# A fused linear attention and gated feed-forward kernel: the written-out order of all engines' operations replaced by another one

## The chip, the cores and the metric

The kernel runs on one core of one Trainium2 chip. The metric is the device time of one execution in microseconds. The core has five engines with a queue of instructions each: PE (TensorE, matrix products from SBUF into PSUM), DVE (VectorE) and ACT (ScalarE), which do elementwise work and empty PSUM, POOL (GpSimd), which here issues the loads, and SP (SyncE), which issues the stores. An engine works through its own queue in order and waits where an operand isn't ready or a buffer isn't free. PSUM has eight banks of 128 x 512 fp32 values.

## The reference

Eight batches with eight heads, 576 positions, head size 64; model width 512, hidden width 1024.

```python
kv = np.einsum('bhsd,bhse->bhde', k, v)
out = np.einsum('bhsd,bhde->bhse', q, kv)
rms = np.sqrt(np.mean(out * out, axis=-1, keepdims=True) + 1e-06)
x = (out / rms * g_norm)            # then heads side by side: (8, 576, 512)
h = np.maximum(x @ w_in, 0.0)       # (8, 576, 1024)
conv_out = cw[0] * h[s-1] + cw[1] * h[s] + cw[2] * h[s+1]   # along the positions
gate = 1.0 / (1.0 + np.exp(-conv_out))
y = (h * gate) @ w_out              # (8, 576, 512)
```

## The kernel before

The program is a list of small operations. `ORDER` (L59) is a string of some 850 tokens; the loop at L779 issues them one after the other, and the last loop (L786) ties every instruction to the one before it on its engine. So the string is the order of each engine's queue. A token is a name, its numbers after dots, and after `@` the buffer or PSUM bank that it takes. Numbers are mostly batch `b`, pair of heads' tiles `u` and half of the positions `s`; for the feed-forward part batch `b` and hidden block `f` (0 to 7); for the output a pair of batches `p` and a block `m` of 128 rows (0 to 8).

PE's operations:
- `fi.n.512` (L283): n fillers, products of zeros with 512 columns that nobody reads. `ct` transposes the constants.
- `qt` (L425) transposes q in 64x64 blocks; `kv` and `kz` (L395, L473) form k-by-v for all heads; `ot` and `ox` (L454, L492) form q-by-kv. All these use PE's array as 64x64 tiles.
- `on` (L524) and `oq` (L531) sum the squares over a head, `on` with the full 128x128 array, `oq` with 64x64 tiles. For batches 4 to 7 this is done by `ss` (L560, 128x32 tiles) for two batches at once, and `sp` (L587, 32x128 tiles) spreads the factors back.
- `hk` (half of the contraction), `hs` and `hm` (L652, L624, L608) form the hidden layer; `cv` (L701) does batch 0's convolution of four hidden blocks as products.
- `om.p.m.f0.4` (L727) adds four hidden blocks to an output block: `om.p.m.0.4` is the first half, `om.p.m.4.4` the second. `oh.3.8.c` (L753) does the last block in two halves of the columns.

What empties PSUM or prepares operands, on ACT or DVE:
- `caa`/`cad` (L392, L389): batch 0's inputs from fp32 to bf16, on ACT or DVE. `qa`/`qd` (L448, L451) copy the transposed q, `kva`/`kvd` (L419, L422) copy kv, `ea`/`ed` (L736, L741) copy an output block, `eh`/`dh` (L765, L770) copy a half of the last one; the first name of each is ACT's, the second DVE's.
- ACT: `sq` squares, `oc` copies o, `nl` and `ln` take the reciprocal root, `rp`, `rh`, `re` are the relu, `sg` and `sc` the sigmoid. Going from a root to a sigmoid or back loads a table (L227).
- DVE: `mo` and `mu` scale by root and g, `sl` splits the factors in bf16 parts, `ta` (two multiplications), `aa`, `ab` form the convolution, `mg` gates. `pl`, `ps`, `pn`, `pc`, `pg`, `dg` prepare constants.

Transfers: `Lq`, `Lk`, `Lv`, `Li`, `Lo` load q, k, v, w_in and w_out through POOL, with a cast; a load into a buffer waits until its last reader is done. k and v have two buffers each, q three. `st` and `sh` store a row block or a half of one through SP; `tq` transposes q by a transfer, and `kx` swaps the halves of kv, both through SP as well. `pre` starts the loads of batch 0 on SP and ACT.

Dependencies between engines come from the data and the buffers alone; each PSUM bank is named in the token, so a product that takes a bank waits for the operation that empties it.

Of the kernel before, what the change touches and what calls it, by code (L numbers as in the profile page):

```python
# [89 lines left out]
nl.3.0.0@4 hs.3.4.1@7 rh.3.4.1 hs.3.1.1@6 rh.3.1.1 on.3.1.0@4 nl.3.1.0@5 mo.3.0.0 hs.3.6.1@7 rh.3.6.1 hs.2.6.0@6  # L90
# [40 lines left out]
mg.7.1.3 om.3.3.0.4@2 om.3.3.4.4 ed.3.3@5 st.3.3 mg.7.1.2 om.3.1.0.4@1 om.3.2.0.4@7 om.3.0.4.4 om.3.2.4.4 ed.3.2@0  # L131
st.3.2 ed.3.0@2 st.3.0 om.3.1.4.4 ea.3.1@1 st.3.1 om.3.4.0.4@0 om.3.5.0.4@4 om.3.6.0.4@3 om.3.7.0.4@6 om.3.7.4.4
ed.3.7@4 om.3.5.4.4 ea.3.5@3 st.3.5 om.3.4.4.4 ed.3.4@5 st.3.4 st.3.7 om.3.6.4.4 ea.3.6@0 st.3.6 oh.3.8.1@1 eh.3.8.1@2
sh.3.8.1 oh.3.8.0@0 eh.3.8.0@1 sh.3.8.0
"""


@with_exitstack
def kernel(
# [46 lines left out]
    T = {}  # L186
# [260 lines left out]
    @op  # L447
    def qa(b, u, s): qc(0, b, u, s)  # L448
# [376 lines left out]
```

## Time and profile before

| | us |
|---|---|
| median of three runs | 177.79 (177.78 to 178.52) |
| span of the profiled execution, first to last instruction | 175.6 |
| PE busy | 167.9 |
| DVE busy | 149.5 |
| ACT busy | 148.9 |

In the lines of the profile a group is: source line, engine, operation, result and operands, count. Times are in microseconds from the start of the span. In a timeline a line has the start, the length and in brackets the idle time of the engine before it, with what ended it; the length includes the emptying of the engine's pipeline, so that two neighbours can overlap, and the distance between starts is the price of one in a row of many. The chain of waits follows the execution back from its last instruction; its pieces don't overlap. PEld is the load of a product's stationary operand.

### The profile page before, as it was taken

Reading aid. Unit: us, or ns where it says so; the run is one execution under the profiler, and the core shown is the slowest. Engines: PE = TensorE matmul, PEld = TensorE weight load, DVE = VectorE, ACT = ScalarE, POOL = GpSimd, SP = SyncE. Lnnn points to the kernel's source line nnn. Section 1 sums busy time; section 2 is a strip of 40 time slices with the busy share of each in tenths; the row PEclk is TensorE's granted clock in tenths of the full one; section 3 lists DMA queues with packets and bytes.
Section 4 is the critical chain, followed back from the end, with each engine's and each line's share of the span. In section 5 each row is a group of like instructions: output and inputs, shape, how many; then the busy total and the mean of one; then the engine's idle time right before and its main releaser. Section 6 shows DMA issues by size and latency. Waiting matters only on the chain.

```text
span 175.6 us, 5070 instructions
## 1 busy us (share of the span) xinstructions
PE 167.9 (96%) x2097; PEld 100.0 (57%) x2114; DVE 149.5 (85%) x290; ACT 148.9 (85%) x268; POOL 22.2 (13%) x35
## 2 busy tenths in 40 slices
PE   7979999999999999999999999999999999999992
PEld 2334766676447677644467764444877744444451
DVE  2796638899688899999999998989999999999950
ACT  2368899999978999999999998999999967676721
POOL 3094512200603013030000000000000000000000
PEclk9999999999999999999999999999999999999999
DMA  5999999999999999999999050330310003064486
GB/s 159 392 323 207 207 207 207 208 208 209 207 241 230 227 207 207 170 182 197 258 181 161 14 134 0 119 123 0 119 63 0 0 0 116 13 239 175 179 304 237
DMA packets 25911, 29.11 MB, mean 166 GB/s; under 512 B 6036, under 2 KB 20384, under 8 KB 25888
## 3 DMA queue, kind: packets, MB, share of 16 engines
q0 software_dynamic: 13296, 14.50, 49.2%
q1 hardware_dynamic: 12048, 13.11, 26.2%
q10 hardware_dynamic: 544, 1.18, 1.7%
q8 instruction: 16, 0.26, 0.6%
q14 instruction: 7, 0.06, 0.1%
HBM read 32.52 MB, written 9.44 MB: 239 GB/s over the span
## 4 chain that ended last, share of the span: by engine, by line
PE 76%; DVE 12%; ACT 5%; DMA 3%; issue 3%; ACTq 0%; DVEq 0%
PE banks L732 32%; PE banks L628 14%; PE banks L613 9%; PE banks L658 4%; DMA stg<-in_v_dram 3%; PE banks L460 3%; DVE h L722 2%; PE banks L708 2%; ACT taps L698 2%; PE banks L402 2%; PE banks L593 2%; PE banks L433 1%; PE banks L528 1%; DVE taps L681 1%; PE banks L286 1%
## 5 line engine op out<-in xcount | busy, mean ns | idle before, releaser
L732 PE MATMUL banks<-w_out_sb,h 128*128 128x512 bf16 x267 | 62.8, 379 | 1.2 <-issue 0.6
L698 ACT ACTIVATE taps<-taps,cw 128x576 bf16<-128x576 bf16 (+1 forms) x44 | 40.6, 958 | 5.7 <-DVE taps L692 5.5
L732 PEld LDWEIGHTS <-h 128*128 128x128 bf16 x280 | 26.2, 98 | 30.0 <-issue 1.1
L628 PE MATMUL banks<-x,w_in_sb 128*128 128x288 bf16 (+2 forms) x256 | 34.2, 286 | 0.0
L640 ACT ACTIVATE h<-banks 128x288 bf16<-128x288 f32 (+2 forms) x80 | 29.5, 460 | 0.3 <-PE banks L658 0.2
L628 PEld LDWEIGHTS <-w_in_sb 128*128 128x128 bf16 x256 | 24.4, 98 | 7.8 <-issue 0.8
L722 DVE TENSOR_TENSOR h<-h,taps 128x1152 bf16<-128x1152 bf16 (+1 forms) x24 | 22.8, 952 | 1.2 <-ACT taps L698 1.2
L687 DVE TENSOR_TENSOR taps<-taps 128x1152 bf16<-128x1152 bf16 (+1 forms) x22 | 21.5, 978 | 0.5
L509 ACT ACTIVATE sq<-banks 128x576 bf16<-128x576 f32 (+2 forms) x32 | 20.8, 691 | 1.1 <-PE banks L460 1.1
L692 DVE TENSOR_TENSOR taps<-taps,h 128x1152 bf16<-128x1152 bf16 (+1 forms) x22 | 21.4, 972 | 0.3
L681 DVE TENSOR_SCALAR taps<-h,cw 128x576 bf16<-128x576 bf16 (+1 forms) x44 | 18.7, 424 | 0.6 <-ACT h L665 0.5
L682 DVE TENSOR_SCALAR taps<-h,cw 128x576 bf16<-128x576 bf16 (+1 forms) x44 | 18.4, 418 | 0.0
L738 ACT ACTIVATE row<-banks 128x512 f32<-128x512 f32 x23 | 13.5, 597 | 5.7 <-PE banks L732 4.2
L658 PE MATMUL banks<-x,w_in_sb 128*128 128x288 bf16 (+2 forms) x128 | 17.7, 286 | 0.1
L613 PE MATMUL banks<-x,w_in_sb 128*128 128x288 bf16 x128 | 16.9, 286 | 0.0
L556 DVE SCALAR_TENSOR_TENSOR x<-banks,cw,rs 128x576 bf16<-128x576 f32 (+2 forms) x16 | 13.0, 816 | 3.9 <-ACT rs L545 3.6
L658 PEld LDWEIGHTS <-w_in_sb 128*128 128x128 bf16 x128 | 12.0, 98 | 4.4 <-issue 0.5
L227 ACT ACT_TABLE_LOAD x10 | 12.8, 1283 | 2.0 <-issue 1.8
L613 PEld LDWEIGHTS <-w_in_sb 128*128 128x128 bf16 x128 | 12.3, 98 | 3.7 <-issue 0.2
L443 DVE COPY qT<-banks 128x1152 bf16<-128x1152 bf16 (+2 forms) x13 | 8.8, 681 | 5.7 <-PE banks L433 5.7
L545 ACT ACTIVATE rs<-banks,eps_sb 128x576 f32<-128x576 f32 (+2 forms) x16 | 11.8, 740 | 1.1 <-PE banks L528 1.1
L599 DVE SCALAR_TENSOR_TENSOR x<-o,cw,banks 128x576 bf16<-128x576 f32 (+2 forms) x16 | 12.1, 810 | 0.7 <-PE banks L593 0.5
(89 smaller groups left out, 162.9 us busy)
## 6 DMA issues: line engine op xcount, KB each, us to landing
out_dram<-row SPq DMA_DIRECT2D x35, 256.0 KB, 2.3
q_sb<-in_q_dram POOLq DMA_DIRECT2D x6, 576.0 KB, 17.9
k_sb<-in_k_dram POOLq DMA_DIRECT2D x6, 576.0 KB, 14.5
v_sb<-in_v_dram POOLq DMA_DIRECT2D x6, 576.0 KB, 17.9
stg<-in_v_dram ACTq DMA_DIRECT2D x2, 576.0 KB, 6.2
stg<-in_k_dram SPq DMA_DIRECT2D x4, 288.0 KB, 6.9
w_in_sb<-in_moe_w_in_dram POOLq DMA_DIRECT2D x2, 512.0 KB, 9.9
w_out_sb<-in_moe_w_out_dram POOLq DMA_DIRECT2D x1, 1024.0 KB, 15.5
```

The costliest lines, as they stand in the source:

```text
L509: nc.scalar.activation(T["sq", b, u, s], T["o", b, u, s], AX.Square)
L613: nc.tensor.matmul(ps[:, s, :HS], w_in_sb[:, t, f * P:(f + 1) * P], T["x", b][:, t, c0:c1], start=(t == 0), stop=(t == NT - 1))
L628: nc.tensor.matmul(ps, w_in_sb[:, t, f * P:(f + 1) * P], T["x", b][:, t, c0:c1], start=(t == 0), stop=(t == NT - 1))
L640: nc.scalar.activation(h, fr, AX.Relu)
L658: nc.tensor.matmul(T[at], w_in_sb[:, t, f * P:(f + 1) * P], T["x", b][:, t, c0:c1], start=(t == 0), stop=(t == NT - 1))
L681: nc.vector.tensor_scalar_mul(tap[:, 0, f % 2, :n, 8:8 + S], h[:, f], cw[:, f:f + 1])
L682: nc.vector.tensor_scalar_mul(tap[:, 1, f % 2, :n, :S], h[:, f], cw[:, 2 * NF + f:2 * NF + f + 1])
L687: nc.vector.tensor_add(tap[:, 1, :, :n, :S], tap[:, 0, :, :n, 7:7 + S], tap[:, 1, :, :n, 1:1 + S])
L692: nc.vector.tensor_add(y, y, span(b, n)[:, 2 * j:2 * j + 2])
L698: nc.scalar.activation(y, y, AX.Sigmoid, scale=cw[:, NF + f:NF + f + 1])
L722: nc.vector.tensor_mul(h, h, tap_of(b, j)[:, 1, :, :n, :S])
L732: nc.tensor.matmul(T["om", p, m], h[:, f, m * P:(m + 1) * P], w_out_sb[:, f, :], start=(f == 0), stop=(f == NF - 1))
```

## The change

`ORDER` is replaced as a whole, and two buffers are made by whichever token comes first instead of by the one with number 0. The set of operations is the same but for these:

- 22 copies and casts change engine. To ACT: `caa.q.0.0`, `caa.v.0.0`, `caa.k.1.0`, `caa.v.3.0`, `caa.q.0.1`, `qa.0.0.0`, `qa.0.1.0`, `kva.3.0.2`, `ea.0.1`, `ea.2.8`, `ea.3.0`, `ea.3.2`, `ea.3.3`, `ea.3.7`. To DVE: `cad.v.1.0`, `cad.q.1.0`, `qd.0.0.1`, `ed.1.0`, `ed.1.1`, `ed.1.4`, `ed.3.5`, `dh.3.8.0`.
- `oq` becomes `on` for 1.0.0 and 1.0.1, and `on` becomes `oq` for 1.1.0 and 3.0.0.
- The fillers go from 37 to 42.

The order of the loads, of the stores and of the transposing transfers is new too, and so are the banks and buffers. The diff, cut to the front, the loads of k for batches 5 and 6, and the end:

```diff
-pre@0,1 af cad.q.0.0@0 cad.v.0.0@0 fi.10.512@0 qt.0.0.0@2 qd.0.0.0@0 gt.k.1.0 Li.0.4 fi.9.512@0 ct@0 Lq.1.0.2@1
-Lk.1.0.2@0 Lv.1.0.2@1 Li.4.4 ps pg fi.4.512@1 cad.k.1.0@1 caa.v.1.0 caa.k.0.0 kv.0.0.1@4 kva.0.0.1@0 ot.0.0.0@6 pc
-cad.v.3.0 cad.k.2.0 fi.2.512@0 cad.k.3.0 caa.q.1.0 qt.0.1.0@2 qd.0.1.0@1 sq.0.0.0@0 oq.0.0.0@4 fi.2.512@0 dg.1
-caa.v.2.0 kv.0.1.1@0 fi.2.512@2 nl.0.0.0@0 kva.0.1.1 ot.0.1.0@4 sq.0.1.0@1 cad.q.0.1 qt.0.0.1@2 qa.0.0.1 fi.2.512@0
-oq.0.1.0@0 nl.0.1.0@1 mo.0.0.0@0 cad.q.1.1 qt.0.1.1@6 qd.0.1.1 mo.0.1.0 ot.0.0.1@2 sq.0.0.1@2 ot.0.1.1@6 fi.1.512@0
-sq.0.1.1@3 oq.0.0.1@0 nl.0.0.1@2 fi.1.512@4 fi.1.512@4 hk.0.1.0.0@4 hk.0.1.0.1 rp.1.0@0 on.0.1.1@0 nl.0.1.1@3
+pre@0,1 af pl ps caa.q.0.0@0 caa.v.0.0@0 fi.20.512@0 qt.0.0.0@0 qa.0.0.0@0 pn caa.k.0.0@0 cad.v.1.0 fi.8.512@2 ct@0 pg
+caa.k.1.0 pc gt.k.1.0 Li.0.4 caa.v.2.0 fi.4.512@1 kv.0.0.1@0 Lq.1.0.2@1 kva.0.0.1@0 cad.q.1.0 caa.v.3.0 fi.2.512@2
+ot.0.0.0@0 dg.0 qt.0.1.0@2 Lk.1.0.2@1 dg.2 sq.0.0.0@0 cad.k.2.0 qa.0.1.0@1 Lv.1.0.2@1 cad.k.3.0 fi.3.512@4 oq.0.0.0@4
+nl.0.0.0@0 dg.3 fi.1.512@6 kv.0.1.1@2 Lq.1.2.2 dg.1 kva.0.1.1 mo.0.0.0@0 caa.q.0.1 Li.4.4 fi.2.512@6 ot.0.1.0@2
+cad.q.1.1 sq.0.1.0@0 fi.1.512@4 qt.0.0.1@4 Lv.1.2.2 qd.0.0.1 oq.0.1.0@6 qt.0.1.1@0 nl.0.1.0@1 Lk.1.2.2 ot.0.0.1@4
+qd.0.1.1 sq.0.0.1@0 ot.0.1.1@0 mo.0.1.0 sq.0.1.1@1 fi.1.512@6 oq.0.0.1@6 nl.0.0.1@0 on.0.1.1@2 nl.0.1.1@1 mo.0.0.1
+hk.0.1.0.0@6 Lq.2.0.4@0 hk.0.2.0.0@7 hk.0.2.0.1 hk.0.1.0.1 mo.0.1.1 rp.2.0@0 hk.0.3.0.0@2 hk.0.3.0.1 rp.1.0
+hk.0.1.1.0@3 Lo.0.8 rp.3.0 hk.0.0.0.0@4 hk.0.2.1.0@5 hk.0.2.1.1 hk.0.1.1.1 rp.2.1 hk.0.0.1.0@7 Lk.2.0.4@0 hk.0.0.1.1
...
-hs.3.3.0@5 rh.3.3.0 rh.3.7.0 kv.4.0.2@0 kvd.4.0.2@1 hs.3.0.0@2 hs.3.3.1@6 mg.1.1.1 Lk.5.0.4@0 rh.3.3.1 hs.3.2.1@7
...
-Lv.5.0.4@1 Lq.7.0.4@1 Lk.6.0.4@1 oc.4.0.0@6 hs.2.7.1@3 rh.2.7.1 ot.4.0.1@0 sq.4.0.1@1 oc.4.0.1@7 kv.5.0.2@4 ta.2.2.0@1
...
+kv.3.0.2@2 sq.2.0.0@0 ed.0.0@3 hk.1.3.0.1 kva.3.0.2@0 Lk.6.0.4@1 on.2.0.0@4 rh.1.3.0 hs.2.5.1@2 nl.2.0.0@0 Lv.5.0.4@1
...
+mo.3.0.0 on.3.1.0@2 rh.3.1.1 hs.3.6.1@5 nl.3.1.0@1 hs.2.3.0@4 mo.3.1.0 kv.4.0.2@2 qt.4.1.0@0 kvd.4.0.2@0 Lk.5.0.4@0
...
+oc.4.0.1@0 aa.2.2.1 om.0.7.4.4 sq.4.0.0@1 hs.3.7.1@2 oc.4.0.0@1 ed.0.7@4 ot.4.1.1@0 rh.2.6.0 kv.5.0.2@6 ta.2.2.0@1
...
+ss.6.6.2@0 ab.4.2.3 ss.7.6.2 om.1.4.0.4@6 ed.1.1@4 ln.6@0 om.1.7.0.4@7 oc.7.0.1@6 sl.6@0 st.1.1 oc.7.1.0@7 om.1.4.4.4
...
-st.3.2 ed.3.0@2 st.3.0 om.3.1.4.4 ea.3.1@1 st.3.1 om.3.4.0.4@0 om.3.5.0.4@4 om.3.6.0.4@3 om.3.7.0.4@6 om.3.7.4.4
-ed.3.7@4 om.3.5.4.4 ea.3.5@3 st.3.5 om.3.4.4.4 ed.3.4@5 st.3.4 st.3.7 om.3.6.4.4 ea.3.6@0 st.3.6 oh.3.8.1@1 eh.3.8.1@2
-sh.3.8.1 oh.3.8.0@0 eh.3.8.0@1 sh.3.8.0
+om.2.4.0.4@1 st.2.0 sg.7.1.4 st.3.0 om.2.4.4.4 mg.7.1.2 om.3.4.0.4@3 ea.2.4@2 st.2.4 om.3.4.4.4 om.3.6.4.4 ed.3.4@1
+om.3.7.4.4 st.3.4 ea.3.6@0 om.3.5.0.4@0 ea.3.7@5 st.3.7 om.3.5.4.4 st.2.3 st.3.6 oh.3.8.0@1 ed.3.5@1 oh.3.8.1@2 st.3.5
+dh.3.8.0@2 st.3.2 sh.3.8.0 eh.3.8.1@3 sh.3.8.1
...
     def kvc(eng, b, u0, n):
-        if u0 == 0:
+        if ("kvb", b) not in T:
...
     def qc(eng, b, u, s):
-        if s == 0:
+        if ("qT", b, u) not in T:
```

More of the change, by code (lines that the diff above doesn't have):

```diff
@@ new lines @@
+om.2.2.0.4@0 ta.6.1.6 sg.6.1.2 aa.6.1.3 om.2.2.4.4 ea.2.1@3 mg.6.1.1 st.2.1 om.2.7.0.4@1 ea.2.2@4 st.2.5 ab.6.1.3
+st.2.2 om.2.7.4.4 ta.7.1.1@1 sg.6.1.7 st.2.8 ta.7.1.0 om.2.6.0.4@0 sg.6.1.6 aa.7.1.0 ea.2.7@2 om.2.6.4.4 mg.6.1.3
+om.3.1.0.4@2 ab.7.1.0 ea.2.6@3 ta.7.1.3@0 om.3.1.4.4 sg.7.1.0 ta.7.1.2 sg.7.1.1 om.3.2.0.4@3 aa.7.1.1 ea.3.1@1
+om.3.2.4.4 mg.7.1.0 st.3.1 st.2.6 ab.7.1.1 om.3.0.0.4@0 ea.3.2@4 st.2.7 ta.7.1.7@1 sg.7.1.3 om.3.0.4.4 ta.7.1.6
+sg.7.1.2 om.2.3.0.4@1 aa.7.1.3 ea.3.0@1 mg.7.1.1 om.2.3.4.4 ab.7.1.3 om.3.6.0.4@0 ea.2.3@3 ta.7.1.4@0 sg.7.1.6
@@ L135 @@
+om.3.3.0.4@1 ta.7.1.5 sg.7.1.7 aa.7.1.2 om.3.3.4.4 ab.7.1.2 om.3.7.0.4@2 ea.3.3@5 mg.7.1.3 sg.7.1.5 st.3.3
+om.2.4.0.4@1 st.2.0 sg.7.1.4 st.3.0 om.2.4.4.4 mg.7.1.2 om.3.4.0.4@3 ea.2.4@2 st.2.4 om.3.4.4.4 om.3.6.4.4 ed.3.4@1
+om.3.7.4.4 st.3.4 ea.3.6@0 om.3.5.0.4@0 ea.3.7@5 st.3.7 om.3.5.4.4 st.2.3 st.3.6 oh.3.8.0@1 ed.3.5@1 oh.3.8.1@2 st.3.5
+dh.3.8.0@2 st.3.2 sh.3.8.0 eh.3.8.1@3 sh.3.8.1
 """
```

118 lines of the change are left out of this document (54 added, 64 removed).

## The prediction

> **What bounds the kernel now.** I read the page first: the shares of the engines and the chain that ended last.
>
> ```profile
> span 175.6 us, 5070 instructions
> PE 167.9 (96%) x2097; PEld 100.0 (57%) x2114; DVE 149.5 (85%) x290; ACT 148.9 (85%) x268; POOL 22.2 (13%) x35
> ...
> PE 76%; DVE 12%; ACT 5%; DMA 3%; issue 3%; ACTq 0%; DVEq 0%
> ```
>
> TensorE (PE) is busy 96% of the span and carries 76% of the chain; VectorE (DVE) and ScalarE (ACT) have 85% each. An average over the span says little of a new order, so I cut it into stages: the front (until the last normalization product of batch 0), three stretches of the body, the last output products, and what follows the last product. Columns: stretch, its length, then busy time and count of each engine, clock, DMA share, GB/s.
>
> ```profile
> 1.20:17.80 16.60, 15.23 (x212) 6.71 (x216) 11.29 (x48) 9.36 (x16) 8.64 (x14) 1.00 1.05 289
> 17.80:60.00 42.20, 41.60 (x760) 27.84 (x762) 32.28 (x73) 39.44 (x79) 9.63 (x13) 1.00 1.21 215
> 60.00:115.00 55.00, 54.25 (x797) 33.45 (x796) 53.01 (x80) 54.36 (x95) 3.70 (x5) 1.00 0.90 152
> 115.00:140.00 25.00, 24.82 (x183) 16.47 (x183) 23.71 (x34) 24.82 (x45) 0.00 (x0) 1.00 0.14 53
> 140.00:172.30 32.30, 32.03 (x158) 15.52 (x159) 28.86 (x58) 20.52 (x38) 0.00 (x0) 1.00 0.41 153
> 172.30:175.60 3.30, 0.00 (x0) 0.00 (x0) 0.00 (x0) 0.36 (x1) 0.00 (x0) 1.00 0.53 188
> ```
>
> Three things are to be seen. PE idles only 0.60 + 0.75 + 0.18 + 0.27 = 1.8 us in the 154.5 us of the body, and 16.60 - 15.23 = 1.4 us in the front: an order can win 3.2 us at most there, since it removes no product. From 60 to 140 us ACT is as full as PE (0.82 us idle of 80). And 3.3 us follow the last product.
>
> **The change part by part.** Array changes first. The order before changes PE's tile (64x64, 32x128 and 128x32 against 128x128) 88 times; I counted the new order in the same way, and it has 88 too, in the same kinds. Their price stands in the chain of waits (start, length, what):
>
> ```profile
> 45.16 0.31 PE banks L433 x36
> 45.47 0.97 PE banks L732 x4
> 46.44 0.24 PE banks L528 x2
> ...
> 49.65 0.86 PE banks L732 x4
> ```
>
> Four output products take 0.86 us, or 0.216 each, between neighbours of the same tile, and 0.97 behind 64x64 work: 0.11 us for a change. 88 against 88 gives 0; one more or fewer would be 0.11.
>
> The operations are the same too, but for the engine of 22 copies and casts, four normalization products that change between the block form (oq) and the full one (on), both of which stream twice 288 columns (0.24 us for two at L528), and the fillers (zero products at L286). These go from 37 to 42.
>
> ```profile
> 1.20 4.45 PE L286 MATMUL banks<-zero 128*128 128x512 bf16 x10 [1.20 <-DVE zero L265]
> ...
> 5.57 0.32 PE L433 MATMUL banks<-ident,q_sb 64*64 64x64 bf16 x16
> ...
> 5.83 2.12 PE L286 MATMUL banks<-zero 128*128 128x512 bf16 x9
> ...
> 8.04 1.04 PE L286 MATMUL banks<-zero 128*128 128x512 bf16 x4
> ...
> 9.01 0.22 PE L402 MATMUL banks<-v_sb,k_sb 64*64 64x64 bf16 x2
> 9.57 0.47 PE L402 MATMUL banks<-v_sb,k_sb 64*64 64x64 bf16 x34 [0.34 <-DVE k_sb L384]
> ```
>
> The first ten take 0.43 us apiece, those after 5.8 us about 0.22 (the product itself 0.216). The new order begins with 20. Ten at 0.43 and ten at 0.22 end at 1.2 + 4.4 + 2.2 = 7.8 us, so the transposes of q that started at 5.57 start 2.2 us later, though q is cast by then. Twenty at 0.22 would have ended at 5.5, just when q is there: the layout seems to count them all at the fast price. Next come 8 fillers, the transposed constants and 4 fillers: 7.8 + 0.25 + 1.8 + 0.2 + 1.0 = 11.05 us for the first k-by-v products, which before started at 9.01 and stalled to 9.57.
>
> What of these 2 us is still there when the front ends? I lay ACT and PE side by side, ACT by the distances between starts in these rows (q cast 0.52, square 0.49, v cast 0.60, root about 0.6):
>
> ```profile
> 10.10 0.28 ACT L416 ACTIVATE kvb<-banks 128x128 bf16<-128x128 f32 x1 [2.55 <-PE banks L402]
> 10.27 0.62 ACT L386 ACTIVATE q_sb<-stq 128x512 bf16<-128x512 f32 x1
> 10.79 0.59 ACT L509 ACTIVATE sq<-banks 128x512 bf16<-128x512 f32 x1
> 11.28 0.68 ACT L386 ACTIVATE v_sb<-stg 128x576 bf16<-128x576 f32 x1
> 11.88 0.69 ACT L545 ACTIVATE rs<-banks,eps_sb 128x512 f32<-128x512 f32 x1
> ...
> 16.86 0.60 PE L658 MATMUL banks<-x,w_in_sb 128*128 128x256 bf16 x4
> ...
> 17.37 0.43 PE L528 MATMUL banks<-sq,ones 128*128 128x320 bf16 x2
> ...
> 17.87 0.78 ACT L545 ACTIVATE rs<-banks,eps_sb 128x640 f32<-128x640 f32 x1
> ```
>
> New order, ACT: its 2.55 us of idle before L416 is filled with the casts of k and v, so kvb is copied at 11.45, the last v cast ends 12.25, sq.0.0.0 12.75, qa.0.1.0 13.25, nl.0.0.0 (waits for PE's oq) 14.0, kva 14.4, the q cast 14.95, sq.0.1.0 15.4, nl.0.1.0 16.45, sq.0.0.1 17.05, sq.0.1.1 17.6, the two roots 18.95. PE: ot.0.0.0 11.95, oq.0.0.0 13.05, kv.0.1.1 13.75, ot.0.1.0 14.7, qt.0.0.1 15.2, oq.0.1.0 15.5, ot.0.0.1 16.05, ot.0.1.1 16.6 (after DVE's qd.0.1.1), oq.0.0.1 17.15, on.0.1.1 17.75 to 18.0. Before, on.0.1.1 ended at 17.8 with four gated-layer products already done (0.44) and three fillers still to come (0.65), so its equal point is 17.8 - 0.44 + 0.65 = 18.0. The front comes out even: the eight more fillers in it (1.75) stand where PE stalled for copies. The layout takes every handover at its shortest; 0.1 more at eight of them is +0.8, and the most that could be won is the 1.4 of idle less the 1.1 of five fillers, -0.3. I take **+0.2**.
>
> [...]
>
> **17.8 to 60 us.** ACT starts this stretch 0.3 late (its second root ends at 18.95, before at 17.87 + 0.78 = 18.65), and gets two copies from DVE: ea.0.1 and kva.3.0.2, 0.48 and 0.3. That is 1.1 us more before the same products against 2.76 of idle (42.20 - 39.44). Queued behind are the squares and roots of batches 1 to 3, and PE waits for their on/oq products. All of it hidden is 0, none is +1.1; the idle is over twice as large, so **+0.3**.
>
> **60 to 140 us.** Three output copies (ed.1.0, ed.1.1, ed.1.4) go to DVE. Prices:
>
> ```profile
> L738 ACT ACTIVATE row<-banks x23: 574/597/653, 47.9 to 170.5; 128x512 f32<-128x512 f32 x23
> L743 DVE COPY row<-banks x12: 681/686/692, 45.0 to 169.6; 128x512 f32<-128x512 f32 x12
> ```
>
> ACT, which has no idle here, loses 3 x 0.60 = 1.8; DVE gets 3 x 0.69 = 2.1 against 2.0 + 1.3 of idle up to 140 us. ed.1.1 stands before sl.6 on DVE, so the factors of batches 6 and 7 (sp, mu) wait behind it; but the new order gives PE its four om.1.4 and om.1.7 halves (3.5 us) meanwhile. The gain is bounded by PE's 0.75 + 0.18 of idle, the loss by the 2.1. Measured against DVE's work up to the mg or mu that they need, the products that had no room before (om.1.6, hm.4.7) stand some 3 us later on PE now, so I take **-0.5**.
>
> **140 us to the last product.** Five output copies go to ACT (ea.2.8, 3.0, 3.2, 3.3, 3.7); ed.3.5 and the half copy dh.3.8.0 go to DVE. ACT idles 32.30 - 20.52 = 11.8 us there, which hides 5 x 0.60; without it they would cost 3.0. PE's idle there is 0.27: **0**, give or take 0.3.
>
> **The tail.** SP issues stores in order, and the transfers are full at the end:
>
> ```profile
> 168.30:171.40 3.10, 3.10 (x21) 1.89 (x20) 0.97 (x2) 1.25 (x3) 0.00 (x0) 1.00 0.93 346
> 171.40:174.30 2.90, 0.79 (x8) 0.46 (x5) 0.00 (x0) 0.72 (x2) 0.00 (x0) 1.00 0.93 334
> 171.76 1.25 SPq L777 DMA_DIRECT2D out_dram<-row  x2
> DMA to landing us min/median/max: 1.9/2.3/7.8
> ```
>
> The new order holds st.2.3 and st.3.2 back, behind stores that wait for fresh rows: st.3.7 can go 2.85 us before the last product ends (eight products at 0.216 and sixteen halves at 0.11 follow its own, less 0.6 for the copy), and behind it stand 2.3, 3.6, 3.5, 3.2 and the two halves: with it 6 x 0.262 = 1.57 MB. At 0.34 MB per us that is 4.6 us. The fastest store lands 1.9 after its issue, 0.8 of it transfer, so 1.1 goes before the data, and the last byte lands 2.85 after the last product; before, transfers ran until 174.3, 2.0 after it. The bounds are 0 (if SP is early) and +0.9; I take **+0.5**.
>
> **Loads.** POOL issues them in a new order. The load of q for batch 2 goes ahead of w_out, and k for batch 5 behind k for batch 6 and v for batch 5; it now takes the buffer of batch 4's k, so its issue waits for kv.4.
>
> ```profile
> 16.87 0.91 POOL L365 DMA_DIRECT2D w_out_sb<-in_moe_w_out_dram  x1 [2.30 <-DMA w_in_sb<-in_moe_w_in_dram]
> ...
> 53.49 0.74 POOL L347 DMA_DIRECT2D k_sb<-in_k_dram  x1 [5.33 <-PE banks L402]
> ...
> 67.96 0.74 POOL L347 DMA_DIRECT2D k_sb<-in_k_dram  x1 [2.52 <-PE banks L402]
> ...
> 73.94 0.75 PE banks L402 x72
> k_sb<-in_k_dram POOLq DMA_DIRECT2D x6, 576.0 KB, 14.5
> ...
> w_out_sb<-in_moe_w_out_dram POOLq DMA_DIRECT2D x1, 1024.0 KB, 15.5
> L732 PE MATMUL banks<-w_out_sb,h x267: 379/379/390, 41.1 to 170.1; 128*128 128x512 bf16 x134
> ```
>
> Before, k of batch 5 was issued at 53.49 and used at 73.94. Now it can go out once kv.4 is done (before 67.9; by the new order some 4 us of PE work earlier, 64), and kv.5 stands 2.6 us of PE work later, at 76.5. At the 215 GB/s of the row for 17.8 to 60 us a load of 0.59 MB takes 2.7 us; at most the two loads issued before it are ahead, so it lands by 64 + 3 x 2.7 = 72.1: cost 0, covered by 4.4 us. w_out landed at 16.87 + 15.5 = 32.4 and was first used at 41.1; behind q it lands at 35.1, and its first product stands some 3 us of PE work earlier, at 38: hidden too, with 3 us to spare.
>
> The sum: +0.2 + 0.3 - 0.5 + 0 + 0.5 + 0 = **+0.5 us** on the 175.6 of the profiled execution, 176.1. Its span is 2.2 us under the median of the runs (177.79), which I take as what lies around it: **178.3 us**.
>
> **The rivals.** *The waits go.* PE's 3.2 us of idle are what the new order was laid out to remove; less five fillers (1.1) that is -2.1, or 175.7; with the tail kept, and a little idle left, 176.4. For it: the consumers of mg and mu stand later than before. Against: ACT has about 1 us less room at every square. Chance 0.26.
>
> *The ten extra fillers are never taken back.* If each handover of the front hangs on the one before it, the 2.0 us by which the first kv is late pass on to the first gated product. The place is the front, the price 2.0 less the 0.2 already counted, the time 178.3 + 1.8 = 180.1. It decides if on.0.1.1 ends later than 18.7. For it: ACT's casts and roots are in one queue. Against: before, PE idled 1.4 us there for copies. Chance 0.24.
>
> *k of batch 5 lands late.* Issued at 64, and landing after the 14.5 us that such a load takes in the median, it is there at 78.5 and kv.5 waits 2.0 us: 180.3. It decides from 12.5 us of flight. For it: the DMA share is 1.21 and 0.90 in these stretches. Against: most of the 14.5 is queueing behind loads that are fewer here. Chance 0.13.
>
> That the change does not do what it says holds for the array changes (88 and 88); it is in the forecast, chance 0.37.
>
> **How the numbers follow.** Slower by over 0.5% (0.9 us, about what a measurement of this kernel can tell from no change) are the two slow rivals, 0.24 + 0.13 = 0.37; faster is the first, 0.26; within, the forecast, 0.37. The unknown terms alone (-0.3 to +0.8, 0 to +1.1, -0.9 to +2.1, 0 to +0.9) do not fall together; half their spread puts the forecast's own range at 177.3 to 179.3. Taking in most of the rivals, 8 in 10 lie in 176.3 to 180.7.
>
> **What would show it.** Right: on.0.1.1 ends between 17.8 and 18.7, the first transposes at 7.8, PE idle 1 to 2 us between there and the last product, and the last store 2.5 to 3 us after it. Wrong: kv.5 idle for k_sb, sq rows with PE behind them near 45 to 50 us, or DVE's sl.6 late for sp.6. Should the first ten fillers take 0.22 us, or the body's idle fall under 0.5 us, the time is under 177.

## The result, and the profile after

| | before | after |
|---|---|---|
| median of the runs, us | 177.81 | 185.25 |
| profiled execution, us | 177.78 | 183.89 |
| its span, us | 175.6 | 181.8 |

The kernel after is slower: the ratio of its runs to those of the kernel before is 1.034, with a 95% interval of 1.031 to 1.037. The four runs of the kernel after spread from 183.8 to 188.8 us, and the ratios, here and below, leave the disturbed ones out, while the medians hold all runs. Everything below explains the 6.2 us between the spans of the profiled executions.

The page of the kernel after: span, PE's row, and the chain of waits by engine.

```profile
span 181.8 us, 5094 instructions
...
PE 171.2 (94%) x2119; PEld 101.1 (56%) x2119; DVE 146.5 (81%) x284; ACT 153.1 (84%) x274; POOL 21.9 (12%) x35
...
PE 81%; DMA 8%; ACT 5%; issue 3%; DVE 1%; SPq 0%; ACTq 0%; DVEq 0%
```

PE is busy for 171.2 instead of 167.9 us, of which five more fillers are 1.1 (17 of the kernel before's 2,114 products have no record, which makes its busy time a little low); transfers (DMA) have gone from 3% of the chain to 8%. The stretches where PE stands still are seen in the view by stretches (length, then busy time of PE, PEld, DVE, ACT, POOL, granted clock, DMA share, GB/s):

```profile
17.80:60.00 42.20, 41.36 (x714) 27.29 (x714) 31.08 (x58) 39.74 (x78) 10.04 (x14) 1.00 1.20 203
60.00:70.00 10.00, 8.21 (x234) 5.93 (x233) 5.98 (x9) 8.41 (x17) 2.22 (x3) 1.00 1.23 200
70.00:90.00 20.00, 19.92 (x329) 11.43 (x326) 19.11 (x32) 19.95 (x42) 1.48 (x2) 1.00 1.19 202
90.00:95.00 5.00, 3.49 (x30) 1.74 (x28) 3.39 (x6) 3.79 (x8) 0.00 (x0) 1.00 1.16 286
95.00:178.00 83.00, 82.17 (x609) 47.89 (x608) 75.69 (x122) 71.17 (x119) 0.00 (x0) 1.00 0.29 93
```

The same view of the kernel before, for the two stretches that differ:

```profile
60.00:70.00 10.00, 9.96 (x218) 7.47 (x210) 9.70 (x19) 9.93 (x21) 2.22 (x3) 1.00 1.21 207
...
90.00:95.00 5.00, 5.00 (x44) 3.82 (x44) 4.86 (x9) 5.00 (x7) 0.00 (x0) 1.00 1.25 94
```

Two holes of 1.8 and 1.5 us in PE's work were not there before, and DVE and ACT fall idle in the same stretches: they wait for PE, not the other way. PE's waits from 20 us on in the kernel after, and below them in the kernel before (what waited and for what: us in total, times, longest):

```profile
PE banks L433 <- issue: 1.8, 1, 1.8
PE banks L500 <- DMA qT<-q_sb: 1.5, 1, 1.5
PE banks L460 <- ACT rs L545: 0.2, 1, 0.2
```

```profile
PE banks L732 <- issue: 0.6, 4, 0.2
PE banks L732 <- DVE taps L692: 0.2, 1, 0.2
```

The first wait of the kernel after has no releaser: PE waited for nothing that the profile shows. It stands in the middle of the transposes `qt.5.0.0`, not at their start (timeline of all engines):

```profile
65.48 0.78 PE L402 MATMUL banks<-v_sb,k_sb 64*64 64x64 bf16 x72
...
66.07 0.70 PE L433 MATMUL banks<-ident,q_sb 64*64 64x64 bf16 x41
...
68.53 0.44 PE L433 MATMUL banks<-ident,q_sb 64*64 64x64 bf16 x31 [1.76 <-issue]
```

The load of their q had landed at 61.7 us by the trace. Here `kv.4.0.2`, `qt.4.1.0` and `qt.5.0.0` follow each other, 288 products and weight loads with some 1.3 us of work. The second wait is that of `ox.6.0.0` for a transposing transfer. SP's queue in the kernel after, and in the kernel before:

```profile
64.62 1.35 SPq L467 DMA_TRANSPOSE qT<-q_sb  x1
66.08 14.77 SPq L748 DMA_DIRECT2D out_dram<-row  x4
80.94 3.85 SPq L467 DMA_TRANSPOSE qT<-q_sb  x1
```

```profile
65.92 2.16 SPq L467 DMA_TRANSPOSE qT<-q_sb  x1
79.87 5.41 SPq L748 DMA_DIRECT2D out_dram<-row  x3
...
86.91 5.98 SPq L467 DMA_TRANSPOSE qT<-q_sb  x2
```

In the kernel before the first one, at 65.92, is `tq.6.0`. In the kernel after the first is `tq.6.1`, and `tq.6.0`, which PE needs first, stands behind four stores. The chain of waits of the kernel after has it (start, length, what):

```profile
80.94 12.34 DMA qT<-q_sb
93.28 0.04 issue
93.33 0.33 PE banks L500 x4
```

The front and the end, in PE's and SP's timeline:

```profile
1.19 6.85 PE L286 MATMUL banks<-zero 128*128 128x512 bf16 x20 [1.19 <-DVE zero L265]
7.97 0.32 PE L433 MATMUL banks<-ident,q_sb 64*64 64x64 bf16 x16
...
11.19 0.48 PE L402 MATMUL banks<-v_sb,k_sb 64*64 64x64 bf16 x36
...
18.52 0.43 PE L528 MATMUL banks<-sq,ones 128*128 128x320 bf16 x2
19.26 0.92 PE L658 MATMUL banks<-x,w_in_sb 128*128 128x256 bf16 x7 [0.32 <-ACT rs L545]
...
175.34 1.91 PE L757 MATMUL banks<-w_out_sb,h 128*128 128x256 bf16 x16
...
177.61 0.82 SPq L777 DMA_DIRECT2D out_dram<-row  x2
```

To add these up I count, for each operation on PE, the work in the queue ahead of it without fillers (0.216 us for a product of 512 columns, 0.12 for 288, 8.5 ns for one of the small 64-column ones, 0.093 for an array change, the spacings of the records) and take it from its start. What is left is the time lost so far:

| at | before, us | after, us | more |
|---|---|---|---|
| first hidden-layer products | 12.87 | 14.82 | 1.95 |
| 40 us of work done | 14.35 | 16.39 | 2.04 |
| 50 | 15.00 | 19.11 | 4.11 |
| 70 | 15.72 | 19.48 | 3.76 |
| 80 | 16.09 | 21.37 | 5.28 |
| last products | 16.44 | 21.50 | 5.06 |
| last product to the landing of the last store | 2.42 | 3.39 | 0.97 |
| from there to the end of the span | 0.96 | 1.18 | 0.22 |

So the front loses 1.95 us, the wait without a releaser 2.1, the transposing transfer 1.5, the stores 1.0, and 0.2 more follow the last store; between these places the new order gives back 0.5. The sum is 6.25.

### The profile page after: what moved, and what is told of

It is laid out like the page before. It is cut to its first block, busy times and chain, and to the rows that moved or that the text cites. A ratio compares the mean times of both kernels' runs of the same rounds, so it can differ in the third digit from the quotient of the medians.

```text
span 181.8 us, 5094 instructions
## 1 busy us (share of the span) xinstructions
PE 171.2 (94%) x2119; PEld 101.1 (56%) x2119; DVE 146.5 (81%) x284; ACT 153.1 (84%) x274; POOL 21.9 (12%) x35
## 3 DMA queue, kind: packets, MB, share of 16 engines
q10 hardware_dynamic: 544, 1.18, 1.7%
## 4 chain that ended last, share of the span: by engine, by line
PE 81%; DMA 8%; ACT 5%; issue 3%; DVE 1%; SPq 0%; ACTq 0%; DVEq 0%
PE banks L732 30%; PE banks L628 17%; PE banks L613 8%; PE banks L658 7%; DMA qT<-q_sb 7%; PE banks L286 6%; PE banks L402 2%; PE banks L433 2%; PE banks L460 2%; ACT sq L509 1%; ACT rs L545 1%; DMA out_dram<-row 1%; PE banks L528 1%; PE banks L537 1%; PE banks L500 1%
## 5 line engine op out<-in xcount | busy, mean ns | idle before, releaser
L732 PE MATMUL banks<-w_out_sb,h 128*128 128x512 bf16 x280 | 64.5, 379 | 0.0
L738 ACT ACTIVATE row<-banks 128x512 f32<-128x512 f32 x25 | 15.1, 602 | 5.8 <-PE banks L732 5.0
L681 DVE TENSOR_SCALAR taps<-h,cw 128x576 bf16<-128x576 bf16 (+1 forms) x44 | 18.7, 425 | 0.4 <-ACT h L640 0.3
L682 DVE TENSOR_SCALAR taps<-h,cw 128x576 bf16<-128x576 bf16 (+1 forms) x44 | 19.0, 431 | 0.0
L443 DVE COPY qT<-banks 128x1152 bf16<-128x1152 bf16 (+1 forms) x12 | 8.4, 711 | 8.8 <-PE banks L433 4.8
L286 PE MATMUL banks<-zero 128*128 128x512 bf16 x42 | 13.0, 449 | 1.2 <-DVE zero L265 1.2
```

Source lines behind the costliest of these rows:

```text
L286: nc.tensor.matmul(ps[:, :w], zero[:, :P], zero[:, :w], start=True, stop=True)
L682: nc.vector.tensor_scalar_mul(tap[:, 1, f % 2, :n, :S], h[:, f], cw[:, 2 * NF + f:2 * NF + f + 1])
L732: nc.tensor.matmul(T["om", p, m], h[:, f, m * P:(m + 1) * P], w_out_sb[:, f, :], start=(f == 0), stop=(f == NF - 1))
```

## The experiments

**What the first wait is.** The records of the transfers hold 16 of 16,384 bytes each (0.26 MB in all) on a queue of instructions, for some 4,240 PE and weight-load instructions. The queue in the page of the kernel after (packets, MB, share of 16 engines):

```profile
q8 instruction: 16, 0.26, 0.6%
```

That is some 265 instructions to a transfer. In the kernel after such a transfer runs from 66.32 to 67.29 us, and PE goes on at 68.53. That gives the first theory: TensorE ran out of instructions. Rivals are an operand, and the order of the body. First I undid one part of the change at a time.

`a_spread_qt`: `qt.5.0.0` later, so that the small products don't follow each other.

```diff
-... Lk.5.0.4@0 qt.5.0.0@6 sg.1.1.5 qd.4.1.0@1 hs.3.0.1@2 Lq.7.0.4@0 sg.1.1.4 hs.3.6.0@3 qd.5.0.0@2 tq.6.1@4 Lv.6.0.4@0 hs.3.2.0@0 rh.3.0.1 mg.1.1.2 ...
+... Lk.5.0.4@0 sg.1.1.5 qd.4.1.0@1 hs.3.0.1@2 Lq.7.0.4@0 sg.1.1.4 hs.3.6.0@3 tq.6.1@4 Lv.6.0.4@0 hs.3.2.0@0 qt.5.0.0@6 rh.3.0.1 mg.1.1.2 qd.5.0.0@2 ...
```

> The kernel after, with qt.5.0.0 three hidden-layer groups later (behind hs.3.0.1, hs.3.6.0 and hs.3.2.0), and its copy qd.5.0.0 with it; nothing else moves. Theory 'instruction supply': PE stands still at 66.77 to 68.53 us inside qt.5.0.0 because kv.4.0.2, qt.4.1.0 and qt.5.0.0 follow each other without a long product between them (227 recorded PE and PEld instructions in 1.2 us; 165 is the most in any 1.2 us of the kernel before), and TensorE has used up the instructions that are loaded; spreading them takes the 1.76 us wait away, the time falls by 1.3 to 1.9 us to about 182.2. Rival 'data': qt.5.0.0 waits for the q of batch 5 or for the transposing transfer tq.6.1 that runs at the same time; then it stands at 68.5 us wherever it is in this stretch, no or little wait is saved before it because the three groups are done first, and a pause of at least 0.2 us stays in qt.5.0.0 if it comes before 68.5; the time falls by at most 0.5.

Measured: median 185.59, ratio 1.041 (1.038 to 1.044). The wait left `qt.5.0.0`, and came back in the long products, 1.1 us at 69.55 (lines are two lower in this kernel):

```profile
PE banks L498 <- DMA qT<-q_sb: 1.8, 1, 1.8
PE banks L626 <- issue: 1.1, 1, 1.1
```

Counted from the first filler it is the same place in both kernels: 2,222 instructions stand ahead of `qt.5.0.0` in the kernel after and the wait comes 11 later; here it comes 11 behind the same 2,222 too, after five long products and six weight loads. All sixteen waits of 1 us and more without a releaser, in the kernel after and in the runs below, stand at about 1,468, 2,234, 2,490, 2,745 or 3,000 instructions, each 184 to 188 past a multiple of 256; that is the block which I count with from here on. The wait belongs to a number of instructions, not to an operation: no operand explains that. My size was wrong, since the block came about as late (its transfer ended at 68.08 us instead of 67.29) although the place of its end had moved.

`a_tq_first`: `tq.6.0` behind `ot.4.0.1`, that is ahead of `st.0.7` and `st.0.1`.

> The kernel after, with the transposing transfer tq.6.0 ahead of the two stores st.0.7 and st.0.1 on SP instead of behind them. Theory 'held-back transfer': in the kernel after it is issued at 80.94 us, 5.7 us after the last reader of its buffer (the q-by-kv products at 74.7 to 75.1 us), lands 12.3 us later at 93.28, and ox.6.0.0 waits 1.5 us for it; issued at about 75.3 it lands before 91.5 even if it takes 14 us, the wait goes, and the time falls by 1.2 to 1.8 us to about 182.3. Rival 'traffic': the transfer is slow because the loads of q, v and k of batches 6 and 7 fill the transfer engines until 92.7 us, it lands with them whenever it is issued, and the wait stays over 1 us: the time falls by less than 0.5 us.

Measured: median 185.95, ratio 1.038 (1.032 to 1.043); the profiled span is 180.7, 1.1 less than after. The transfer is issued at 75.12 and `ox.6.0.0`, at 92.17, no longer waits:

```profile
75.12 1.84 SPq L467 DMA_TRANSPOSE qT<-q_sb  x1
...
91.08 1.15 PE L628 MATMUL banks<-x,w_in_sb 128*128 128x288 bf16 x8
92.17 0.33 PE L500 MATMUL banks<-qT,kvb 64*64 64x320 bf16 x4
```

The wait is explained. The profiled execution gained what the wait had cost, but the runs as a whole did not get faster.

`a_stores_early`: `st.3.2` behind `st.2.7`, `st.2.3` behind `ea.3.3`.

> The kernel after, with st.3.2 and st.2.3 issued on SP when their rows are copied (behind st.2.7 and behind ea.3.3), not among the last stores. Theory 'stores held back': after the last product the kernel after needs 4.55 us to its end, the kernel before 3.4, because two whole rows of 256 KB are queued in front of the two last half rows; with them out of the way the end comes 0.7 to 1.2 us earlier, about 183.0. Rival: the last half row is late by its own copy and store alone, and the time stays within 0.3 us.

Measured: median 185.12, ratio 1.037 (1.033 to 1.041). From the last product to the landing of the last store it took 2.55 us instead of 3.39, as expected; but the profiled run had a second late block, which took the gain:

```profile
79.65 0.53 PE L628 MATMUL banks<-x,w_in_sb 128*128 128x288 bf16 x3 [3.05 <-issue]
```

`a_fill10`: `fi.20.512@0` becomes `fi.10.512@0`.

> The kernel after, with 10 fillers instead of 20 ahead of the first transpose, as in the kernel before. Theory 'fillers': the first transpose starts at 7.97 us though its q is cast at 5.56; without ten fillers it starts at about 5.6, the first hidden products at about 17.5 instead of 19.26, and the time falls by 1.2 to 2.1 us to about 182.2. Rival 'casts on ACT': ACT, which has five more casts and copies of batch 0 than before, sets the pace of the front, the first hidden products start at 18.7 or later, and the time falls by less than 0.6 us.

Measured: median 185.23, ratio 1.038 (1.034 to 1.042). The hidden layer begins at 17.12 instead of 19.26 us. Then it is all given back in a wait that ends at 47.82:

```profile
47.82 0.41 PE L433 MATMUL banks<-ident,q_sb 64*64 64x64 bf16 x26 [2.10 <-issue]
```

So the fillers do cost 2.1 us at their place, and ACT's casts don't set the front. But 20 instructions fewer in front move all block ends by 20, and a block with 2.79 us of work arises where the kernel after has one of 4.08 (a wait of 0.29).

**Where the blocks are cut.** `a_cut` leaves the body alone and cuts fillers into smaller products:

```diff
-fi.20.512@0 ... fi.8.512@2 ... fi.4.512@1 ... fi.3.512@4
+fi.40.256@0 ... fi.32.128@2 ... fi.16.128@1 ... fi.12.128@4
```

> The kernel after, with the fillers of the front cut into smaller products of the same sum of columns (75 products of 512, 256 and 128 columns more or less instead of 35; 130 PE and PEld instructions more ahead of everything else, no other change). Theory 'instruction blocks': TensorE's instructions arrive in blocks of 256 (the 16384-byte transfers of the instruction queue, 16 in each kernel), one block ahead, and a block that is used up in less than about 4.4 to 4.9 us waits for the next; in the kernel after the block that holds kv.4.0.2, qt.4.1.0 and most of qt.5.0.0 has only 2.85 us of work (and stands 1.76 us at 68.53), the one with kv.2.0.2 and qt.3.0.0 4.08 us (0.29 us). With 130 more instructions in front the blocks are cut elsewhere, the shortest has 4.9 us, both waits go though no operation of the body has moved: 1.7 to 2.1 us less, about 182.0. Rival 'data': the wait belongs to the operands of qt.5.0.0 or to the burst itself wherever the blocks begin; PE stands still there as before, 183.5 to 184.5.

```profile
66.01 0.95 PE L433 MATMUL banks<-ident,q_sb 64*64 64x64 bf16 x72
66.89 4.09 PE L628 MATMUL banks<-x,w_in_sb 128*128 128x288 bf16 x32
```

The same 72 transposes now run through without a wait. The rival fails at this place, yet the median is 188.03, ratio 1.042 (1.037 to 1.047). In the profiled execution (188.58 us) `tq.6.0` landed at 95.3 us, and `ox.6.0.0` waited 3.9 us for it; two of the six runs were below 187, at 184.57 and 186.03. `b_cut` does the same to the kernel before:

```diff
-fi.10.512@0 ... fi.9.512@0 ... fi.4.512@1
+fi.20.256@0 ... fi.36.128@0 ... fi.16.128@1
```

> The kernel before, with three of its groups of fillers cut in the same way (98 PE and PEld instructions more, the same columns). Theory 'instruction blocks': the cuts now fall so that one block of the body has 3.15 us of work and another 4.17 (4.68 was the shortest); PE stands still at their ends for 1.2 to 1.8 and 0.2 to 0.7 us, which the kernel before never does: 179.2 to 180.2. Rival 'data' or 'new order': the kernel before keeps its order and its operands, so it stays at 177.5 to 178.3.

Measured: median 183.11, ratio 1.030 (1.027 to 1.032), more than expected. PE waits 2.87 us, up to 78.12, where one block has 3.15 us of work. Then it is slow: from the three output products at 78.91 to the next start at 80.32 it takes 1.41 us, where 0.216 each and an array change make 0.74 (the mean granted clock of this execution is 0.988):

```profile
PE banks L460 <- issue: 2.9, 1, 2.9
PE banks L732 <- issue: 0.8, 4, 0.3
```

The kernel before has no such wait; 98 more instructions in its front, for the same columns of fillers, make one.

**Repairs together.** `a_fill10_cut` is 10 fillers with a cut that leaves no block under 5.0 us of work.

> The kernel after with 10 fillers instead of 20 ahead of the first transpose, and the fillers cut so that the shortest block has 5.0 us. In the uncut kernel with 10 fillers the front was 2.1 us earlier and gave it back in one wait of 2.1 us at 45.7 to 47.82 us, where the block that ends there has 2.79 us of work. Theory 'instruction blocks': without that wait and the one at 68.5 the front's 2.1 us and the 2 us of the waits both stay gained, 179.6 to 180.4. Rival 'loads': the body is held by loads that land at fixed times (v of batch 2 at 40.9, q of batch 3 at 43.8 us), so that a shorter front is given back by 48 us whatever the blocks are: 181.6 or more.

Measured: median 187.93, ratio 1.056 (1.053 to 1.060). By 65.4 us only 15.6 us were lost (after: 19.1), so neither loads nor the order hold the body up to there. Then k of batch 5 came at 82.9 us:

```profile
PE banks L402 <- DMA k_sb<-in_k_dram: 6.8, 1, 6.8
```

The kernel after loads k of batch 6 ahead of v and k of batch 5 and doesn't feel it, because it is late itself. `a_mend` adds the repairs of `a_tq_first` and `a_stores_early`:

> The kernel after with all four edits: 10 fillers in front, the fillers cut as in the run before this one, tq.6.0 ahead of the two stores, st.3.2 and st.2.3 issued when their rows are ready. If the four causes add up to the loss (front 2.0, instruction blocks 2.0, transposing transfer 1.5, stores 0.9 us, and 5.06 us of PE time and 1.1 us behind it to be found): 177.0 to 178.3, level with the kernel before. Rival 'the order of the body itself is worse' (ACT's longer list, the array changes): at least 1 us stays, 179 or more.

Median 187.11, ratio 1.047 (1.042 to 1.052): the same wait, 5.4 us, and a block 2.0 us late at 71.66, although the cut left it 5.0 us of work. `a_k5_swap` is the kernel after with two pairs of transfers exchanged:

```diff
-Lk.6.0.4@1 ... Lk.5.0.4@0 ... tq.6.1@4 ... Lk.7.0.4@0 ... tq.6.0@0
+Lk.5.0.4@1 ... Lk.6.0.4@0 ... tq.6.0@4 ... Lk.7.0.4@1 ... tq.6.1@0
```

> The kernel after with the order of two pairs of transfers set back to that of the kernel before: k of batch 5 is loaded where k of batch 6 was and the other way round (buffers exchanged too), and tq.6.0 takes the place and buffer of tq.6.1 and the other way round. Front, blocks and stores stay as in the kernel after. Theory 'transfers': ox.6.0.0 no longer waits (its transposing transfer is issued at about 64.6 us instead of 80.94), the 1.5 us of that wait go, and with it most of the drops of TensorE's clock to half for 3.4 us that follow it in the disturbed runs: 182.0 to 182.7. Rival: the wait moves on to ox.6.1.1, or the loads behind the exchanged transfer land later and kv.5.0.2 or kz.6.0.2 waits instead: 183.5 or more.

Median 183.87, ratio 1.035 (1.032 to 1.038). `ox.6.0.0` doesn't wait; `kz.6.0.2` waits instead, for v of batch 6, which landed at 90.1 (after: 82.3):

```profile
PE banks L433 <- issue: 1.9, 1, 1.9
PE banks L479 <- DMA v_sb<-in_v_dram: 1.4, 1, 1.4
```

`a_mend2` has all of it (10 fillers, cut, transfers, stores), `a_mend3` also issues `tq.6.1` behind `kx.6`.

> All edits together: the transfers of the run before this one, 10 fillers ahead of the first transpose, the fillers cut so that no block has less than 5.0 us, st.3.2 and st.2.3 issued early. In the earlier mended kernel the front and the blocks had gained 3.4 us by 65.4 us, and a wait of 5.4 us for k of batch 5 (landed at 83.2 us, needed at 77.9) took it back. Theory 'four causes and the load order': with k of batch 5 loaded ahead of k of batch 6 it lands by 68 us, no wait is left, and the time is 176.8 to 178.5. Rival 'the transposing transfers slow all loads': k, v of batch 6 land after 88 us and kz.6.0.2 waits 2 us or more: 179.5 to 182.

> All edits together as in the second mended kernel, but tq.6.1 issued behind kx.6 as in the kernel before, so that one transposing transfer runs among the loads instead of two. There the loads of k, q and v of batches 6 and 7 landed 1 to 9 us later than in the kernel before and two blocks of instructions came late (3.8 and 1.8 us). Theory 'transposing transfers hold up loads and instruction blocks': v of batch 6 lands by 86 us, the wait at kz.6.0.2 goes and the time falls to 178 to 182. Rival 'the new order is denser in 66 to 80 us whatever the transfers': its blocks there have 5.0 to 6.3 us of work against 5.2 to 7.7 in the kernel before, a wait of 3 us or more stays there: 183 or more.

Medians 185.91, ratio 1.045 (1.042 to 1.049), and 184.75, ratio 1.036 (1.033 to 1.040). In the first, blocks came 3.8 and 1.8 us late; in the second v of batch 6 landed at 90.9 us and PE waited 4.2 us for it. My theory for `a_mend3` failed: one transposing transfer among the loads instead of two did not bring v earlier.

**Parts of the change put into the kernel before.** `b_k6_first` loads k of batch 6 ahead of v and k of batch 5, `b_fill20` has `fi.20.512@0`.

> The kernel before with the load order of the kernel after at this place: k of batch 6 ahead of v and k of batch 5 (buffers exchanged), nothing else. Theory 'k of batch 5 late': it lands at about 76.6 us, where q of batch 7 landed, kv.5.0.2 needs it at 73.8, and PE waits 2.5 to 3.5 us, with or without a drop of the clock behind it: 180 to 183. Rival: the loads have slack, 177.5 to 178.5.

> The kernel before with 20 fillers instead of 10 ahead of the first transpose. Its shortest block keeps 4.9 us. Theory 'fillers cost what they hold back': the first transpose moves from 5.57 to 7.9 us, the whole front with it, and nothing behind gives it back: 179.6 to 180.3. Rival 'the front has slack' (the step of the prediction that priced the fillers at 0.2 us): 177.6 to 178.3.

Medians 185.44, ratio 1.040 (1.036 to 1.044), and 182.65, ratio 1.025 (1.021 to 1.028). The load order alone costs the kernel before a wait of over 6 us, twice what was expected, since k of batch 5 landed at 80.2 us and not at 76.6:

```profile
80.26 1.17 PE L402 MATMUL banks<-v_sb,k_sb 64*64 64x64 bf16 x72 [6.24 <-DMA k_sb<-in_k_dram]
```

The ten fillers put the hidden layer 2.2 us later and nothing gives it back; besides, a block came 2.4 us late at 76.7. `b_fill20_256` tells whether that is the cut: the same columns, but exactly 256 instructions more than before, so that every block begins where it did.

> The kernel before with the columns of 20 fillers instead of 10 ahead of the first transpose, and its fillers cut so that there are exactly 256 PE and PEld instructions more than in the kernel before: every block of 256 begins and ends at the same operation of the body as in the kernel before. With 20 uncut fillers (20 instructions more) the kernel before took 5 us more: 2.1 in the front, 2.55 in one wait for a block at 74.18 to 76.73 us, the rest at half clock behind it. Theory 'where the blocks are cut': the wait goes although everything still runs 2.1 us later against the loads; 179.5 to 180.3. Rival 'timing against the transfers': the body runs 2.1 us later as with 20 fillers, meets the same transfers and waits the same 2 to 3 us: 181.5 or more.

Median 185.0, ratio 1.030 (1.026 to 1.034). Even the lowest of the six runs, 182.14, is 1.8 us above the range of the theory, and in the profiled execution (185.82 us) the wait is still there, and larger:

```profile
PE banks L628 <- issue: 4.4, 1, 4.4
```

So the cut isn't all: the blocks begin at the same operations as in the kernel before, which has no wait without a releaser over 0.2 us, and some 2 us later against the loads one of them came 4.4 us late. The transfers under way then could be the reason; `b_cut_tq` asks whether it is the transposing transfer.

> The kernel before with its fillers cut (98 instructions more), in which PE waited 3.16 us at 74.96 to 78.12 us for a block with 3.15 us of work, and the transposing transfer tq.6.0 behind the stores, ahead of kx.6, instead of ahead of them, so that it isn't under way then. Theory 'the transposing transfer makes the block late': the wait at about 75 us falls to under 1.7 us (4.4 to 4.9 less 3.15). Rival 'the loads alone': it stays at 2.5 us or more. In both ox.6.0.0 then waits for the late transfer, so the time itself (183 to 190) decides nothing.

Two runs, median 182.73, ratio 1.028 (1.023 to 1.034). Counted as in the expectation the wait at 75 us fell from 3.2 us in `b_cut` to 2.2 (idle time 2.9 and 1.9):

```profile
PE banks L460 <- issue: 1.9, 1, 1.9
```

That lies between the two expectations, from one profiled execution of each, so the transposing transfer is part of it at most.

**The loads taken away.** Without the loads of batches 6 and 7 the last load lands by 69 us in the kernel before and by 73 us in the kernel after. These kernels leave batches 6 and 7 of the output out of the computation, but PE has the same products to do, on the operands of batch 5.

```diff
...
 def load(x, b, t0, n):
+    if b in (6, 7):
+        slots.clear()
+        return
```

> The kernel before without the six loads of q, k and v of batches 6 and 7 (their products read batch 5's buffers, so batches 6 and 7 of the output are left out of the computation). It waits for none of these loads on PE, so theory 'late arrivals' and its rival agree here: 176.3 to 177.8. It is the measure for the two runs beside it.

> The kernel after without the same six loads (batches 6 and 7 of the output left out of the computation). Theory 'late arrivals': of the 6.2 us, the wait for the transposing transfer (1.5 us) goes, since nothing crowds it, and the late block at 66 to 68.5 us is cut to under 1 us because the transfers are done by about 71 us; what is left is the front (2.0 us) and the stores (0.8 us): 3 to 4.5 us above the kernel before without these loads, 180 to 182. Rival 'the body's new order is slower by itself': 5.5 us or more above it.

> As the run before this one (batches 6 and 7 of the output left out of the computation), and with 10 fillers ahead of the first transpose, the fillers cut so that the shortest block has 5.0 us, and st.3.2 and st.2.3 early. If front, blocks, transposing transfer and stores are all of the loss, it is within 1 us of the kernel before without these loads: 176.5 to 178.5. Rival: 2 us or more above it, then the order of the body itself costs something that the shown causes don't hold.

| kernel | median, us | ratio to before | span, us |
|---|---|---|---|
| `b_noload67` | 177.43 | 0.999 (0.998 to 1.000) | 175.7 |
| `a_noload67` | 180.62 | 1.015 (1.014 to 1.017) | 179.4 |
| `a_noload67_ft` | 177.92 | 1.002 (1.000 to 1.003) | 176.1 |

PE's waits in `a_noload67` (lines are up to seven higher here), where no load is in the way:

```profile
PE banks L739 <- issue: 0.3, 2, 0.2
PE banks L665 <- ACT rs L552: 0.3, 1, 0.3
PE banks L600 <- ACT h L647: 0.2, 1, 0.2
PE banks L467 <- ACT rs L552: 0.2, 1, 0.2
```

Both holes are gone although the order, the transposing transfer behind the stores and the cuts are those of the kernel after: the block and the transposing transfer came late because of the loads. 3.2 us are left between the medians, and with 10 cut fillers and early stores 0.5. So with these loads away the new order of the body is slower by 0.5 us at most. With all loads in place no set of repairs showed that: the best median among them is 183.87 (`a_k5_swap`).

## Why the prediction was wrong

The forecast was 178.3 us, within 0.5% of before; the runs are 3.4% slower, above the top of the range.

- Array changes, 88 against 88, at 0: consistent. With the waits away the kernels differ by 0.5 us.
- The front, +0.2: wrong. The start of the transposes (7.8, measured 7.97) and of kv (11.05, measured 11.19) was right; the step that failed is "the front comes out even". It laid each handover of the chain at its shortest, and the lag grew from 0.18 us at `ot.0.0.0` (11.95, measured 12.13) to 0.77 at `on.0.1.1` (17.75, measured 18.52), which ended at 18.95: 0.95 past the equal point of 18.0, and past the bound of +0.8. The 1.95 of the table is this 0.95, the 0.32 us that PE then waited for ACT's second root, and 0.65 of three fillers that the kernel before still has to come, which the prediction had put on its side. The rival "the ten extra fillers are never taken back" had the mechanism, the price (2.0) and the mark (18.7), and got 0.24.
- 17.8 to 60 us, +0.3: the table adds only 0.1 by 40 us of work, but the kernel before passes its three fillers here, so in the prediction's terms the stretch cost 2.04 - 0.95 = 1.1, at the upper bound. Of that 0.32 is the wait for the second root, 0.2 another wait for a root and 0.29 a block that came late at 47.87; the rest is not located.
- 60 to 140 us, -0.5: this is the step that failed most. Its bounds were "PE's 0.75 + 0.18 of idle" for a gain and 2.1 of DVE's copies for a loss; the loss from the front to 80 us of work was 3.3, and of PE's waits in it only 0.2 us was for ACT and none for DVE. Two suppliers of PE that were not in the sum were late: the blocks of instructions (2.1) and `tq.6.0` (1.5). The second could have been read: the prediction counted the copies that change engine, but not the transposing transfers that change places on SP, past stores that wait for rows.
- 140 us to the last product, 0: right; from 80 us of work to the last products the loss fell by 0.2.
- The loads, 0: `kv.5.0.2` did not wait, as forecast, but the 4.4 us of cover were not there. k of batch 5 was issued at 66.7, not 64, and landed at 76.6, not 72.1; the kernel after began `kv.5.0.2` at 79.0 only because of the earlier waits. The rival "k of batch 5 lands late" is what `b_k6_first` and `a_fill10_cut` met.
- The tail, +0.5 (2.85 us from the last product to the last byte): measured 3.39 against 2.42 before, +0.97, just past its upper bound of +0.9. The mechanism was right, 0.8 of it shown by `a_stores_early`; the size was too small.
- The rival "the waits go" (0.26) failed too: even with the loads of batches 6 and 7 away and the front and the end repaired, the new order took 177.92 us against 177.43.

What stays open is the time of a block. The kernels without six loads show that it depends on the loads (no wait without a releaser over 0.2 us in `a_noload67`, 1.8 in the kernel after), and `b_cut_tq` suggests that one transposing transfer alone doesn't make it; which transfer holds a block up, and how, was not tried further. Each loss was taken away at its place by a run of its own, but all of them together only without those loads.

## What to carry to other kernels

An order laid out with traced durations of the engines' operations has to carry what the engines are fed by as well: each load and transposing transfer with its place in its queue, and the instructions themselves. Where thousands of small products run while loads fill the transfer engines, count the instructions: in these runs 256 of them with 2.8 to 4.1 us of work were a wait of 0.3 to 2.9 us while loads ran (the kernel after, `a_fill10`, `b_cut`), and some with 5.0 to 7.5 us of work waited 2.0 to 4.4 us (`a_mend`, `a_stores_early`, `b_fill20_256`). And a part that is undone alone may show its gain at its place and no gain at the end, since an earlier PE only meets the next late arrival; take the arrivals away to see what an order is worth.

## What the hardware showed

- PE's instructions came in blocks of 256, one block ahead. The sixteen waits of 1 us and more stand 184 to 188 past a multiple of 256, and the records of the kernels before and after hold 16 transfers of 16,384 bytes each. From the moment when PE entered a block (counted by the products ahead, at 186 past the multiple) the transfer began 0.8 to 5.0 us later in these two kernels while loads ran, which was until 92.6 us, and after that from 4.0 us earlier to 1.3 us later. It lasted 0.9 to 2.3 us. In the kernel after PE entered a block at 63.66, the transfer ran from 66.32 to 67.29, and PE went on into the next block at 68.53, 1.24 us after its end; in `a_spread_qt` it went on 1.47 us after it (68.08 and 69.55).
- TensorE's clock fell to about half after one wait of 1.85 us and did not after one of 1.5 and one of 3.05 us. `a_spread_qt` waited 1.85 us up to 94.56, and the view by stretches has the granted clock, the number behind POOL's busy time:

```profile
92.00:95.60 3.60, 1.75 (x18) 0.91 (x17) 1.65 (x3) 2.10 (x6) 0.00 (x0) 1.00 1.19 283
95.60:99.10 3.50, 3.50 (x18) 1.72 (x17) 2.95 (x4) 3.50 (x5) 0.00 (x0) 0.51 1.22 229
```

  These 3.5 us at a granted clock of 0.51 cost about 1.7 us more than the wait, by an estimate from this row alone (3.5 x 0.49). The 1.5 us wait of the profiled kernel after, at the same place, had no such fall (granted clock 1.00 from 90 to 178 us), and neither had the 3.05 us of `a_stores_early` that ended at 79.65: the seven output products behind it, from 80.23 to 81.75, took 0.217 us apiece. So the length of the wait alone doesn't decide.
- A transposing transfer of 128x1152 bf16 values (295 KB) landed 3.2 us after its issue at 101.06 us in the kernel before and at 107.13 in the kernel after, with no load under way since 92.6, and 7.0 to 14.3 us after its issue among the loads of these two kernels (five of them, issued from 64.62 to 89.08).
